# Scaling turned features in place of weights, with the projection in row-split runs and a new order of the prologue

## The chip, the cores and the metric

The kernel runs on one core of a Trainium2 chip. The metric is the device time of one execution in microseconds (us). A run of the changed kernel always has runs of the kernel before beside it on the same chip. PE is the matrix engine, DVE the vector engine, ACT the scalar engine, POOL the general engine, and SP the engine that issues the transfers.

## The reference, cut to what matters

One transformer block with linear attention, S = 2048 tokens, D = 576, 32 heads of 18, hidden width 4608:

```python
mod = (silu(c) @ w_mod).reshape(1, 6, 1, -1)         # sa, ca, ga, sb, cb, gb
h = layernorm(x) * (1 + ca) + sa
q, k, v = h @ wqkv                                   # cut: the split into heads
phi(u) = [softmax(u @ w_phi), softmax(-u @ w_phi)]   # per head, 18 + 18 features
kv, z = sum_s phi(k) v, sum_s phi(k)
o = (phi(q) kv) / (phi(q) z + 1e-6)
x = x + ga * (o @ wo)
h = layernorm(x) * (1 + cb) + sb
x = x + gb * (relu(h @ w1) @ w2)
```

The layer norm's factor (1 + ca) can be put into the weights of K, Q and V, or into the features that they multiply. That choice is the heart of the change.

## The kernel before

The sixteen token tiles of 128 rows pass a *prologue* (modulation, K, V, kv, Q, attention of the first two tiles) and then eight *blocks* of two tiles, each with a first layer (L1, `w1`) and a second layer (L2, `w2`). The prologue is one hand-written order of small jobs, which gives every engine its queue:

```python
ORDER = """
Z11 sx sd rp sc FK ca Z2 fs0 fsr frr fra2 sh frd4 fra0 fra1 bn1 fs3 bn0 fs1 Z1 fra3 shc sa0 wsd2 KR:0 fsd4 fs2
...                                                                            # cut
"""
```

`Zn` is n filler matmuls on zeros; `sc` and `sh` are the modulation's scale and shift products; `FK` folds `w_phi` into K's weights; `fs`, `fsd`, `fr` copy the fold out, scaled or raw; `ws` scales V's weights. The modulation products have one-column matmuls, and `idle` puts a filler in front of every five:

```python
def mods(w, outs, width, bank, idle=None):
    o = PS[:, bank, :] if isinstance(bank, int) else bank[:, 0, :]
    for k, wm in enumerate(w):
        for ci in range(NC):
            if idle is not None:
                spin(1, idle)
            for ck in range(NC):
                pe.matmul(o[0:width, k * NC + ci:k * NC + ci + 1], lhsT=wm[0:R, ck, ci * width:(ci + 1) * width],
                          rhs=siluc[0:R, ck:ck + 1], start=(ck == 0), stop=(ck == NC - 1))
# ...
"sc": lambda: mods([wsc], None, R, 7, idle=6),
"sh": lambda: mods([wsh], None, R, 7, idle=6),
```

Inside the blocks, hooks put the next block's attention between the matmuls:

```python
def in_l1(g, u):
    if not more:
        return
    if (g, u) in ((0, -1), (0, 1)):            # finish a query tile, fetch a later one
        q = t0 + max(u, 0)
        q_fin(q)                               # POOL steps, then the query's turning transfer
        if q + NL < NT:
            q_in(q + NL)
    if (g, u) in ((1, 2), (2, 1)):             # attention, then its turning transfer
        ...
def in_l2(pos):
    if pos in (1, 4): ...                      # projection, ten matmuls; residual; statistics
    if pos in (2, 6): ...                      # second norm; h's turning transfer
    if pos == 12:
        hb = h2[:, (b + 1) % 2]
        for ci in range(NC):
            dve.tensor_scalar(out=hb[:, ci, :], in0=hb[:, ci, :], scalar1=mod2[:, 1, ci:ci + 1],
                              scalar2=mod2[:, 0, ci:ci + 1], op0=ALU.mult, op1=ALU.add)
```

The softmax here doesn't subtract the row's maximum and nothing guards it: scores larger than these inputs give would overflow.

## Time and profile before

| | before |
|---|---|
| median of 3 runs | 393.02 us (391.85 to 393.25) |
| span of the profiled run | 390.7 us |
| PE busy | 383.8 us, 98% |
| first layer of block 0 starts (chain of waits) | 93.68 us |
| a block, from first layer to first layer | 37.05 us, all seven alike |
| last block's start to the end | 37.67 us |

The span is thus three pieces: 93.68 + 7 x 37.05 + 37.67 = 390.7 us.

### The profile page before, as it was taken

To read this page: it belongs to the slowest core of one execution; us is meant where nothing else is said; L and a number is where in the kernel's file an instruction comes from. 1 tells how busy PE (TensorE), PEld (TensorE's weight loads), DVE (VectorE), ACT (ScalarE), POOL (GpSimd) and SP (SyncE) were. 2 spreads that over 40 slices of the span, in tenths; PEclk is the share of its full clock that TensorE was granted. 3 is DMA by queue.
4 is the path that set the end of the run, shared out by engine and by line. 5 is a ranking of instruction groups with operands and counts; after the bars stand their busy time and mean duration, and the time that the engine had idled before them with its cause. 6 is when DMAs were issued, how large, how long until landed. Compare 5 with 4: busy or idle time off the path is not lost.

```text
span 390.7 us, 8908 instructions
## 1 busy us (share of the span) xinstructions
PE 383.8 (98%) x3693; PEld 311.7 (80%) x3693; DVE 244.3 (63%) x452; ACT 157.9 (40%) x360; POOL 142.3 (36%) x199
## 2 busy tenths in 40 slices
PE   8999999999999999999999999999999999999995
PEld 4778888878887888788888878887888788878874
DVE  0889998854879746573755567458555664653221
ACT  1798779699531233124213510531143123312510
POOL 2155858741101510740164045306510641072045
PEclk9999999999999999999999999999999999999999
DMA  7999739795732151125313311450143124010001
GB/s 291 418 420 403 274 133 354 178 306 161 189 65 35 47 121 20 35 61 109 35 27 83 80 35 32 107 65 19 47 93 35 24 69 51 18 34 33 3 0 32
DMA packets 49515, 44.36 MB, mean 114 GB/s; under 512 B 39361, under 2 KB 42050, under 8 KB 48706
## 3 DMA queue, kind: packets, MB, share of 16 engines
q1 hardware_dynamic: 49186, 43.59, 39.6%
q8 instruction: 29, 0.48, 0.5%
q10 hardware_dynamic: 288, 0.19, 0.2%
q14 instruction: 12, 0.10, 0.1%
HBM read 27.97 MB, written 6.49 MB: 88 GB/s over the span
## 4 chain that ended last, share of the span: by engine, by line
PE 86%; POOL 6%; ACT 2%; DVE 2%; DMA 2%; issue 1%; SPq 0%; POOLq 0%; DVEq 0%; ACTq 0%
PE PS L683 33%; PE PS L742 29%; PE PS L274 9%; PE PS L410 5%; PE PS L690 5%; POOL wo_sb L637 2%; PE PS L235 2%; PE PS L391 1%; ACT RT L279 1%; POOL RH L754 1%; DMA gatd<-gt 1%; PE PS L324 1%; POOL RT L291 1%; DMA ga_row<-gatd 1%; DVE st L240 1%
## 5 line engine op out<-in xcount | busy, mean ns | idle before, releaser
L683 PE MATMUL PS<-h,R 128*128 128x256 bf16 x1152 | 133.5, 273 | 0.0
L683 PEld LDWEIGHTS <-R 128*128 128x128 bf16 x1152 | 109.8, 98 | 17.5 <-issue 5.1
L742 PEld LDWEIGHTS <-RH 128*128 128x128 f16 x864 | 84.5, 98 | 21.8
L728 POOL TENSOR_TENSOR yt<-yt,gb_row 128x288 f32<-128x288 f32 x23 | 16.8, 731 | 167.0 <-DVE yt L727 167.0
L742 PE MATMUL PS<-R,RH 128*128 128x288 bf16 (+1 forms) x576 | 75.6, 286 | 0.0
L697 ACT ACTIVATE RH<-PS 128x256 f16<-128x256 f32 x72 | 27.7, 384 | 114.0 <-PE PS L690 107.4
L699 DVE SCALAR_TENSOR_TENSOR RH<-PS,RH 128x256 f16<-128x256 f32 x72 | 30.1, 419 | 68.2 <-ACT RH L697 68.2
L279 ACT ACTIVATE RT<-PS,rs 128x576 bf16<-128x576 f32 x64 | 43.0, 750 | 7.5 <-PE PS L274 7.1
L698 ACT ACTIVATE RH<-PS 128x512 f16<-128x512 f32 x72 | 42.9, 595 | 7.8 <-PE PS L683 6.5
L746 ACT ACTIVATE RS<-PS 128x288 f32<-128x288 f32 x24 | 9.9, 411 | 75.9 <-PE PS L742 75.9
L742 PE MATMUL PS<-RT,RH 128*128 128x288 f16 x288 | 37.9, 286 | 0.0
L274 PE MATMUL PS<-RH,R 116*128 116x288 bf16 x240 | 31.8, 286 | 0.5 <-ACT RH L631 0.5
L754 POOL TENSOR_TENSOR RH<-RH,RT 128x2304 f16<-128x2304 f16 x7 | 31.8, 4548 | 0.0
L274 PE MATMUL PS<-RH,RT 116*128 116x288 bf16 x240 | 31.7, 286 | 0.0
L274 PEld LDWEIGHTS <-R 116*128 116x128 bf16 x240 | 22.9, 98 | 6.4 <-issue 0.7
L274 PEld LDWEIGHTS <-RT 116*128 116x128 bf16 x240 | 22.7, 98 | 5.5
L420 DVE TENSOR_SCALAR xn<-x_sb,mv,rs 128x576 bf16<-128x576 bf16 (+1 forms) x28 | 22.4, 842 | 7.3 <-ACT rs L415 7.3
L729 POOL TENSOR_TENSOR x_sb<-yt,x_sb 128x288 bf16<-128x288 f32 x31 | 22.8, 737 | 5.9 <-DVE yt L725 4.1
L240 DVE BATCH_NORM_STATS2 st<-x_sb 128x6 f32<-128x288 bf16 x60 | 24.2, 445 | 0.5
L410 PE MATMUL PS<-wo_sb,oT 128*128 128x288 bf16 x160 | 22.6, 286 | 0.2 <-POOL wo_sb L637 0.2
L284 DVE TENSOR_REDUCE Rk<-RT 128x64 f32<-128x1152 bf16 x16 | 21.2, 1332 | 1.4 <-ACT RT L279 1.4
L284 DVE TENSOR_REDUCE Rq<-RT 128x64 f32<-128x1152 bf16 x16 | 21.5, 1342 | 0.0
(115 smaller groups left out, 414.2 us busy)
## 6 DMA issues: line engine op xcount, KB each, us to landing
R<-in_w1a_dram SPq DMA_DIRECT2D x4, 1152.0 KB
eqd<-RT SPq DMA_DIRECT2D x14, 288.0 KB, 5.8
RT<-eqd SPq DMA_DIRECT2D x14, 288.0 KB, 2.7
R<-in_w2a_dram SPq DMA_DIRECT2D x3, 864.0 KB, 10.4
R<-in_w2b_dram SPq DMA_DIRECT2D x2, 1296.0 KB, 10.9
out_dram<-x_sb SPq DMA_DIRECT2D x15, 144.0 KB, 3.3
RT<-in_xT_dram SPq DMA_DIRECT2D x2, 640.0 KB
x_sb<-in_xk_dram SPq DMA_DIRECT2D x3, 288.0 KB
```

The lines of the kernel that those rows point to most:

```text
L240: dve.bn_stats(out=s[:, hf, :], in_=x_sb[:, t, hf * HD:(hf + 1) * HD])
L274: pe.matmul(pr[:, k, 0:HD], lhsT=xt(t, ck), rhs=w[0:R, ck, k * HD:(k + 1) * HD], start=(ck == 0), stop=(ck == NC - 1))
L279: act.activation(out=E.rearrange("p (b h s e) -> p b h s e", b=2, s=2, e=DH)[:, :, :, s, :], in_=pr[:, :, 0:HD].rearrange("p b (h e) -> p ...
L284: dve.tensor_reduce(out=Rr, in_=E.rearrange("p (c e) -> p c e", e=DH), axis=AXX, op=ALU.add)
L410: pe.matmul(pr[:, k, 0:HD], lhsT=oT[:, t % 2, ci, :], rhs=wo_sb[:, ci, k * HD:(k + 1) * HD], start=(ci == 0 and not add_x), stop=(ci == NC ...
L683: pe.matmul(PS[:, 2 * u + hf, n * 256:n * 256 + 256], lhsT=w1a[:, ci, jj * P:(jj + 1) * P], rhs=hb[:, ci, :], start=(n == 0 and ci == 0), ...
L697: act.activation(out=A11[:, j, :], in_=lo[:, :, 0, :], func=ACT.Relu)
L698: act.activation(out=A2[:, j, :, :], in_=PS[:, 2 * u + 1, :].rearrange("p (n s f) -> p n s f", n=2, s=2), func=ACT.Relu)
L699: dve.scalar_tensor_tensor(out=U3[:, j, :], in0=lo[:, :, 1, :], scalar=0.0, in1=A11[:, j, :], op0=ALU.max, op1=ALU.subtract)
L729: pool.tensor_tensor(out=x_sb[:, t, c], in0=y, in1=x_sb[:, t, c], op=ALU.add)
L742: pe.matmul(PS[:, bank, 0:HD], lhsT=am[:, j, :], rhs=bm[:, j, :], start=first and j == 0, stop=(j % 9 == 8), skip_group_check=True)
L754: pool.tensor_tensor(out=A12, in0=A12, in1=U2, op=ALU.subtract)
```

## The change

The intent: fewer small operations ahead of K (features are scaled in place of weights), ten projections in each of which two of ten matmuls are replaced by a pair of half-height ones that run at the same time, no identity matmuls for the residual, a last epilogue in two halves, and a new order throughout. The diff, cut to its core:

```diff
 ORDER = """
-Z11 sx sd rp sc FK ca Z2 fs0 fsr frr fra2 sh frd4 fra0 fra1 bn1 fs3 bn0 fs1 Z1 fra3 shc sa0 wsd2 KR:0 fsd4 fs2
+Z11 sx sd rp sc bn1 Z2 ca bn0 FK sa0 sp0 fra0 frd4 sh fra3 frr fra1 xd0 T0:2 fra2 Z2 bn3 Tc0 Ka0:0 shc bn2
 ... (all lines of the order are new)
-    def mods(w, outs, width, bank, idle=None):
+    def mods(w, width, bank):
             for ci in range(NC):
-                if idle is not None:
-                    spin(1, idle)
 ...
+    def x_scale(t, eng):                        # the turned features of two tiles, times 1 + ca
 ...
+            if (g, u) in ((0, 0), (0, 2)):      # in_l1, blocks 2 to 6
+                attend(t0 + u // 2)
+            if g and u == "rest":
+                wo_rest(t0 + g - 1, pair(3))    # the pair of 64-row matmuls, in an existing row-split run
+            if g and u == 0:
+                wo_full(t, pair(3))             # eight full matmuls
+                add_res(t, pair(3))
 ...
+                if b and (g, u) == (1, 0):      # in_l1, block 1
+                    q_next(t0 + 2)
 ...
+            if b > 1 and pos in (4, 9) or b == 1 and pos == 9:   # in_l2
+                q_next(t0 + 2 + pos // 9)
 ...
+        if b + 1 == NB:                         # last epilogue: in halves
+            dve.tensor_tensor(out=yl[:, H4:HD], in0=PS[:, Z, H4:HD], in1=SS[:, 1, H4:HD], op=ALU.add)
+            dve.tensor_copy(out=yl[:, 0:H4], in_=SS[:, 1, 0:H4])
+            pool.tensor_tensor(out=yl, in0=yl, in1=gb_row[:, HD:D], op=ALU.mult)
+            pool.tensor_tensor(out=yl, in0=yl, in1=x_sb[:, t, HD:D], op=ALU.add)
+            dve.tensor_tensor(out=yt[:, 0, c], in0=PS[:, bank, c], in1=gb_row[:, g], op=ALU.mult)
+            dve.tensor_tensor(out=x_sb[:, t, g], in0=yt[:, 0, c], in1=yl[:, c], op=ALU.add)
```

The fillers inside the two modulation products are gone, and the preparation of later query tiles (`q_next`) has moved from the start of L1 into L2 in blocks 2 to 6, while block 1 has two such steps more than before.

## The prediction

> **What bounds the kernel now.** I read first the page's busy table and its slices, for the engine that is never idle; then the windows by stage, for whether that holds in every stage; then the chain that ended last, for what one unit of work costs on that engine; last the timeline of the first 15 us and of the last 5 us, where the slices show holes.
>
> From the page (busy us, share, instructions; then tenths in 40 slices):
>
> ```profile
> span 390.7 us, 8908 instructions
> ...
> PE 383.8 (98%) x3693; PEld 311.7 (80%) x3693; DVE 244.3 (63%) x452; ACT 157.9 (40%) x360; POOL 142.3 (36%) x199
> ...
> PE   8999999999999999999999999999999999999995
> ```
>
> Only the first and last slices have PE below nine tenths. The windows by stage (PE, PEld, DVE, ACT, POOL busy, clock, DMA share, GB/s) agree:
>
> ```profile
> 14.10:30.00 15.90, 15.09 (x178) 12.42 (x179) 14.59 (x28) 13.83 (x36) 7.56 (x21) 1.00 1.02 421
> 30.00:58.00 28.00, 28.00 (x342) 22.83 (x341) 26.88 (x50) 21.54 (x58) 17.63 (x45) 1.00 0.68 264
> ...
> 76.00:93.50 17.50, 17.31 (x167) 14.02 (x165) 11.17 (x23) 16.54 (x31) 6.58 (x5) 1.00 0.76 248
> 93.50:387.00 293.50, 293.29 (x2730) 240.26 (x2727) 171.25 (x320) 86.90 (x201) 94.33 (x91) 1.00 0.27 56
> ```
>
> From 93.5 to 387 us, three quarters of the span, PE lacks 0.2 us and the clock is full: there only PE work that is removed can pay. Before that DVE (26.88 of 28.00) and ACT (16.54 of 17.50) run close behind it.
>
> Busy PE is no proof of a tight stream, so I checked rates in the chain of waits (start, length, what, count):
>
> ```profile
> 167.78 3.06 PE PS L683 x28
> 170.84 0.76 PE PS L690 x12
> ...
> 188.05 1.23 PE PS L410 x10
> 189.28 3.31 PE PS L742 x27
> ```
>
> A 256-column matmul takes 3.06/28 = 0.109 us, a 288-column one 3.31/27 = 0.123 us. The row-split run (L690, twelve matmuls on 64 rows, so six pairs) takes 0.76 = 6 x 0.109 + 0.10 us. One block, 130.73 to 167.78, is 37.05 us; its items add up to that.
>
> The opening has the holes. PE and DVE timeline:
>
> ```profile
> 13.04 0.38 PE L235 MATMUL PS<-zero 128*128 128x512 bf16 x1
> 14.16 1.40 PE L268 MATMUL PS<-R,RS 116*100 116x288 bf16 x10 [0.75 <-DVE RS L614]
> ...
> 13.89 0.13 DVE L614 CAST RS<-PS 116x5 bf16<-116x5 f32 x1
> ```
>
> The first useful dense matmuls (K's bias rows) start at 14.16, behind a DVE queue that was full from 10.5 us: two evictions of the fold's rest (L618, L620), one raw fold (L453), then two layer-norm statistics.
>
> **What the Trainium skill says.** "TensorE: Matmul & The Clock Gate", section Back-to-back issue gap, gives N/2.4 + 2.5 ns for a warm isolated stream: 109.2 ns at N = 256, 122.5 at 288. The trace agrees (109, 123). The same section says that 128-column matmuls with their weight loads sustain only about 81 ns; the trace differs: the 25 fold matmuls of 126 columns take 1.46 us, 58 ns each, so I use the trace. "TensorEngine Tiling (Array Packing)", section Key Properties, says a change of tiling mode drains the engine, while tiles of one mode run in parallel; the 0.10 us excess above is that, and it says why the new projection remainder is put inside an existing row-split run. "VectorE: DVE Perf Modes", section The perf-mode tier table, puts a bf16 scalar multiply from SBUF at 4x and any PSUM source at most at 2x: here the 116x576 SBUF scale (L519) ran three in 0.93 us, the 116x504 PSUM scale (L444) took 0.73 us. That favours scaling features in SBUF.
>
> **The change, part by part.** (1) Scaling the turned features in place of the weights. Removed: of K's fold the scaled copies (four ACT at 0.65-0.68, one DVE at 0.73, one DVE remainder at 0.53), five V scalings on DVE (0.3 to 0.37 each), five scaled Q copies on ACT (0.73 each). Added for eight pairs of tiles: two on DVE (5 x about 0.2-0.35, between a 116x576 scale and L820's 1.78/5 for 256 columns: 1 to 1.8 us a pair), three on ACT (5 x about 0.4 = 2 us, from L697's 0.384 for 256 columns) and three on POOL (1280 elements; L291's 576 take 1.17 us and L754's 2304 take 4.5, so 2.5 us). In total ACT is about even (-6.3 + 6), DVE loses about 3 us and gains 2 to 3.6, and POOL, with room, gains 7.5. PE does no less. What counts is the start. My walk in queue order: the modulation weights land at 6.1 as before; the early token tile lands 0.7 us behind (288 KB at 410 GB/s), so statistics run on a DVE that today has only three tiny operations before 9.07; the 25 scale matmuls without idle fillers end near 7.9 in place of 8.9. The fold's weights land 0.7 us later than they did, near 8.6, so the fold stays at about 8.9 to 10.4. ACT then copies four fold chunks in 2.3 us, to about 12.7; K's first four chunks run to 13.2-13.8; the bias rows start near 13.7 (before 14.16). The half-row evictions let tile 1's exponentials start near 17.2, where the first started at 18.44. Then ACT and DVE feed PE: by my walk PE is about 0.6 us ahead at 27 us. I take 0.6 us from here.
>
> (2) The end of the prologue. Four identity matmuls with the residual go: 4 x 0.123 = 0.49 us of PE. Two ACT copies back to SBUF (0.65 each) go, in a stage where ACT is at 16.54 of 17.50; DVE gets two adds at 0.75 with room. The gate row is sent earlier, so the wait of the first projection for POOL's weights (0.35 us from 82.28 to 82.63) should go. Against that stand three filler matmuls after K's start (3 x 0.22), which I expect inside waits. Sum of PE work from 14.16 to 93.52: 77.2 us counted (480 projections x 0.1225 = 58.8, the rest kv, folds, rows, turns), elapsed 79.4; so 2.2 us of stalls are all that better order can win there. I take 0.6 + 0.49 + 0.35 = 1.4 us together.
>
> (3) Projection in row-split runs, for tiles 6 to 15: ten matmuls of 0.123 become eight, plus one parallel pair of 0.123 without a new mode change. Saved: 0.123 x 10 = 1.23 us, all on the path. For blocks 2 to 6 the attention and projection move from the second layer into the first. Room: attention's output is ready about 5.7 us into the block, its turning DMA takes 2.6, so it lands near 8.5; the first use is at 10.5. The bank pair is read out by DVE about 1.3 us before the second layer writes it. No stall expected, and none removed, since there is none.
>
> (4) The tail. From the timeline:
>
> ```profile
> 384.42 2.37 PE L742 MATMUL PS<-R,RH 128*128 128x288 bf16 x18
> ...
> 386.89 0.46 DVE L777 TENSOR_TENSOR yt<-PS,gb_row 128x288 f32<-128x288 f32 x1 [1.75 <-PE PS L742]
> 387.49 0.46 DVE L778 TENSOR_TENSOR x_sb<-yt 128x288 bf16<-128x288 f32 x1
> ```
>
> The last 18 matmuls become 36 of 144 columns (36 x 62.5 ns = 2.25 us, +0.05). The first half's DVE pair hides under the second half; what is left exposed is two operations on 144 columns at about 0.31 us (0.46 less 144/0.96 ns). 1.06 us becomes about 0.75. Net 0.3 us. The 2.7 us of the last store stay.
>
> Sum: 1.4 + 1.23 + 0.3 = 2.9 us; with a little for order effects that I did not count, 3.3. 393.0 - 3.3 = 389.7.
>
> **Rivals.** First, the front is bound by the loads: DMA share is 1.0 from 4 us on, and loading x earlier only pushes the fold's weights back. For it: the fold already starts as its weights come. Against: DVE, not DMA, ended the last wait (L614). Then the prologue gains only (2), some 0.8 us, and the time is about 390.6. Second, feature scaling becomes a new wait: DVE is 96% busy from 30 to 58, ACT gets three times 2 us in the same stretch, and a POOL scale of 2.5 us stands in front of the small POOL steps (L594, L598) on which V's eviction waits. PE would stall some 1 to 2 us: 391 to 392. Third, the tight end: the last turned tile now stands only one projection (1.23 us) before the first layer; its evictions need 1.0 us on DVE, and on ACT they queue behind a tile's exponentials (1.3 us). That costs up to 0.7 us once. Fourth, the projection waits for its turning DMA inside the first layer: at 1 us a tile over ten tiles that would be +10 us, the only road to slower; the 2 us of room speaks against it. Fifth, upward: the start comes a full 2 us earlier and all stalls go; then 3 + 2.2 + 0.49 + 1.23 + 0.3 = 7.2 us at the very most.
>
> **Range and chances.** Low end 387.4: the start 1.5 us better than my walk and most stalls gone. High end 391.5: rivals one to three in part. Faster by over 2% means under 385.2, a gain of 7.8, beyond the 7.2 that I can find: 0.04. Slower by over 2% needs the fourth rival: 0.02.
>
> **What would show it.** Right: the first-layer stage of block 0 starts near 92 us (93.5 before); blocks 2 to 6 last 36.8 us where they lasted 37.05; in those blocks the second and third row-split runs last about 0.88 us in place of 0.76; last PE to end shrinks by 0.3; PE still lacks under 0.5 us in the blocks. Wrong: idle PE ended by ACT or POOL on the feature tiles between 15 and 58 us (second rival), idle ahead of L690's successor ended by the turning DMA (fourth), or K's first matmul no earlier than before (first). A gain above 6 us would mean stalls that busy PE hides and that my count of 2.2 missed.

## More of the kernel before

In the timeline of PE before (start, length, engine, line, operation, count), the one-column products (L251) alternate with fillers (L235), and the dense fold (L438) follows:

```profile
7.74 0.38 PE L251 MATMUL PS<-siluc,R 116*116 116x1 bf16 x5
7.98 0.38 PE L235 MATMUL PS<-zero 128*128 128x512 bf16 x1
...
8.89 1.58 PE L438 MATMUL PS<-RS,R 126*116 126x126 bf16 x25
```

## The result

The changed kernel takes 398.75 us (median of 4 runs, 397.67 to 399.26), the kernel before in the same rounds 392.51 us. The ratio is 1.0155, with a 95% interval of 1.0123 to 1.0187. Ratios here are the mean time of one kernel's runs over that of the other's of the same rounds, so not quite the ratio of the medians. A gain of 3.3 us was predicted and a loss of 6.2 us came: within 2%, but 7 us above the range.

From the page after, the busy table and two rows of the slices (PE busy, and the clock that PE was granted, in tenths):

```profile
span 397.2 us, 8949 instructions
...
PE 386.0 (97%) x3700; PEld 312.9 (79%) x3701; DVE 237.1 (60%) x463; ACT 157.1 (40%) x376; POOL 146.5 (37%) x202
...
PE   7999999999999998999999999999999999999996
...
PEclk8599999999999999999999999999999999999999
```

PE is as busy as before. The row to look at is the last one: the second slice (9.9 to 19.9 us) has half the clock, where before has nines throughout. Put into the three pieces by the starts of the first layers in the chain of waits:

| piece | before | after | difference |
|---|---|---|---|
| to the first layer of block 0 | 93.68 | 96.34 | +2.66 |
| block 0 | 37.05 | 37.29 | +0.24 |
| blocks 1 to 6 | 222.30 | 225.88 | +3.58 |
| last block and end | 37.67 | 37.69 | +0.02 |
| span | 390.7 | 397.2 | +6.5 |

Of blocks 1 to 6, block 1 lost 1.40 us, block 2 lost 0.53 and the others 0.40 to 0.42 each.

**The opening.** PE's timeline after, which answers to the one of before:

```profile
5.98 1.49 PE L247 MATMUL PS<-siluc,R 116*116 116x1 bf16 x25 [0.69 <-DMA R<-in_wsc_dram]
...
8.54 2.80 PE L432 MATMUL PS<-RS,R 126*116 126x126 bf16 x25 [0.50 <-DMA R<-in_wkT_dram]
11.14 2.63 PE L247 MATMUL PS<-siluc,R 116*116 116x1 bf16 x25
```

The same 25 fold matmuls take 2.80 us in place of 1.58 in this view, and in the window 8 to 17 us the mean granted clock is 0.50 (before 1.00) at almost the same busy time of PE, 8.28 against 8.25 us of 9.00. A busy share does not show a slow clock.

**Blocks 2 to 6.** The chain of waits after, at the start of block 3 (start, length, what, count):

```profile
207.93 1.79 DVE h L857 x3
...
210.57 2.89 PE PS L671 x25
```

Three of the 28 first-layer matmuls have run; the other 25 wait for DVE, which scales the five parts of h. Before, the whole run starts unhindered. In the timeline after, and then in that of before:

```profile
205.64 1.17 POOL L287 TENSOR_TENSOR RT<-RT,ratq 128x576 bf16<-128x576 bf16 x1
...
207.93 2.85 DVE L857 TENSOR_SCALAR h<-h,mod 128x256 bf16<-128x256 bf16 x5
...
208.22 0.73 POOL L717 TENSOR_TENSOR yt<-yt,gb_row 128x288 f32<-128x288 f32 x1
...
209.03 1.41 POOL L718 TENSOR_TENSOR x_sb<-yt,x_sb 128x288 bf16<-128x288 f32 x2
...
209.49 0.67 PE L671 MATMUL PS<-h,R 128*128 128x256 bf16 x3
```

```profile
240.16 1.78 DVE L820 TENSOR_SCALAR h<-h,mod 128x256 bf16<-128x256 bf16 x5
...
240.32 0.77 POOL L729 TENSOR_TENSOR x_sb<-yt,x_sb 128x288 bf16<-128x288 f32 x1 [0.64 <-DVE yt L725]
...
241.72 3.22 PE L683 MATMUL PS<-h,R 128*128 128x256 bf16 x28
```

The five scalings took 2.85 us where they took 1.78, although nothing about them changed. What changed is POOL beside them: two query steps (L287), moved into L2, have pushed POOL's later work (L717, L718) under the scalings. The views of the two lines give the single scalings (min, median and max in ns), before and then after:

```profile
L820 DVE TENSOR_SCALAR h<-h,mod x5: 334/335/761, 240.2 to 241.6; 128x256 bf16<-128x256 bf16 x5
L857 DVE TENSOR_SCALAR h<-h,mod x5: 339/764/885, 207.9 to 210.4; 128x256 bf16<-128x256 bf16 x5
```

By itself a scaling takes about 0.34 us. Before, one POOL instruction (240.32) runs beside the five, and one scaling takes 0.76. After, three POOL instructions do, and three scalings take 0.76 to 0.89. Each of these long scalings ends 0.08 us after a POOL instruction ends. The same holds for all 137 scalings of over 0.6 us at the block ends of the 13 profiled runs that have them on DVE. So DVE stands until the POOL instruction is over, and even the old 1.78 us holds one such wait. This agrees with the Trainium skill, "SBUF — State Buffer", section "SBUF: two separate sides": DVE, when it uses both of its ports, and POOL lock one shared pair of ports for a whole instruction each, and the other blocks. The longest case is in both kernels: h's normalisation (128x576), 0.42 us by itself, takes 2.68 beside POOL's multiplication of 4.55 us (at 233.96 before, at 164.16 after); before, it cost PE nothing.

The new projection itself works as designed. Its waits aside, three undisturbed matmuls take 3 x 0.109 = 0.33 us from 209.49, so the other 25 could start at 209.82; they start 0.75 us later. Blocks 3 to 6 last 37.45 to 37.47 us: 0.75 lost and 0.34 gained on 37.05.

**Block 1.** SP's queue, from the timeline after (SP issues in the order written):

```profile
147.25 1.89 SPq L346 DMA_TRANSPOSE RE<-RT  x1
...
151.19 0.33 SPq L335 DMA_DIRECT2D RT<-eqd  x1
151.61 2.04 SPq L399 DMA_TRANSPOSE oT<-o_sb  x1
```

The attention output `o_sb` is complete at 147.41 us (DVE's last operation on it starts at 146.65 and lasts 0.76). Its turning could have been issued then; it was issued at 151.61, after a query's turning and a fetch into the same buffer that has to wait for that turning. PE pays at the projection:

```profile
155.12 1.40 PE L404 MATMUL PS<-wo_sb,oT 128*128 128x288 bf16 x10 [1.22 <-DMA oT<-o_sb]
```

The Trainium skill, "Perfetto Trace Analysis", section "DMA Instruction — HWDGE (DVE, Sync)", places the wait for semaphores in the issuing sequencer, which is free for the next instruction only after it has issued. The trace agrees: 4.2 us of delay for a transfer whose data was ready. The late projection has a sequel: h's own turning lands late for block 2, at 171.27 us in the chain of waits, and DVE starts to scale h only at 171.37, 0.55 us before the first layer's first matmul, where blocks 3 to 6 have 1.56. That goes with block 2's 0.53 us.

**The tail.** The timeline of DVE after, for the last epilogue in halves:

```profile
393.29 0.31 DVE L774 TENSOR_TENSOR yt<-PS,gb_row 128x144 f32<-128x144 f32 x1 [1.67 <-POOL x_sb L718]
...
394.20 0.31 DVE L775 TENSOR_TENSOR x_sb<-yt,RE 128x144 bf16<-128x144 f32 x1
```

The first half did not hide under the matmuls of the second: it writes the scratch `yt[:, 0]`, which POOL (L718) still reads, so all four operations stand at the end.

### The profile page after: what moved, and what is told of

It is laid out like the page before. It is cut to its first block, busy times and chain, and to the rows that moved or that the text cites. A ratio compares the mean times of both kernels' runs of the same rounds, so it can differ in the third digit from the quotient of the medians.

```text
span 397.2 us, 8949 instructions
## 1 busy us (share of the span) xinstructions
PE 386.0 (97%) x3700; PEld 312.9 (79%) x3701; DVE 237.1 (60%) x463; ACT 157.1 (40%) x376; POOL 146.5 (37%) x202
## 4 chain that ended last, share of the span: by engine, by line
PE 83%; POOL 4%; DVE 4%; DMA 4%; ACT 2%; issue 2%; SPq 0%; POOLq 0%; DVEq 0%
PE PS L671 32%; PE PS L731 24%; PE PS L270 12%; PE PS L678 5%; DVE h L857 3%; PE PS L804 3%; PE PS L404 2%; PE PS L387 2%; DMA R<-in_wkT_dram 2%; ACT RT L275 1%; POOL RH L743 1%; PE PS L320 1%; DMA h<-xn 1%; PE PS L247 1%; POOL RT L287 1%
## 5 line engine op out<-in xcount | busy, mean ns | idle before, releaser
L671 PEld LDWEIGHTS <-R 128*128 128x128 bf16 x1152 | 111.1, 98 | 19.0 <-issue 5.9
L731 PEld LDWEIGHTS <-RH 128*128 128x128 f16 x846 | 82.8, 98 | 20.8
L717 POOL TENSOR_TENSOR yt<-yt,gb_row 128x288 f32<-128x288 f32 x23 | 16.8, 729 | 187.4 <-DVE yt L716 187.4
L731 PE MATMUL PS<-R,RH 128*128 128x288 bf16 (+1 forms) x558 | 72.4, 286 | 0.0
L687 DVE SCALAR_TENSOR_TENSOR RH<-PS,RH 128x256 f16<-128x256 f32 x72 | 28.8, 413 | 62.8 <-ACT RH L685 62.8
L270 PE MATMUL PS<-RH,R 116*128 116x288 bf16 x240 | 33.8, 291 | 0.1
L716 DVE TENSOR_TENSOR yt<-PS,RS 128x288 f32<-128x288 f32 x23 | 10.4, 452 | 29.7 <-POOL RH L743 24.0
L238 DVE BATCH_NORM_STATS2 st<-x_sb 128x6 f32<-128x288 bf16 x64 | 25.9, 447 | 3.6 <-DMA x_sb<-in_xk_dram 3.1
L718 POOL TENSOR_TENSOR x_sb<-yt,x_sb 128x288 bf16<-128x288 f32 x31 | 22.4, 730 | 2.4 <-DVE yt L714 0.6
L678 PE MATMUL PS<-h,R 64*128 64x256 bf16 x288 | 19.9, 271 | 0.0
```

What stands on the lines that cost most here:

```text
L238: dve.bn_stats(out=s[:, hf, :], in_=x_sb[:, t, hf * HD:(hf + 1) * HD])
L270: pe.matmul(pr[:, k, 0:HD], lhsT=xt(t, ck), rhs=w[0:R, ck, k * HD:(k + 1) * HD], start=(ck == 0), stop=(ck == NC - 1))
L671: pe.matmul(PS[:, 2 * u + hf, n * 256:n * 256 + 256], lhsT=w1a[:, ci, jj * P:(jj + 1) * P], rhs=hb[:, ci, :], start=(n == 0 and ci == 0), ...
L678: pe.matmul(PS[:, 2 * u + hf, n * 256:n * 256 + 256], lhsT=w1b[b0:b0 + 64, j * P:(j + 1) * P], rhs=hb[b0:b0 + 64, 4, :], start=False, stop ...
L687: dve.scalar_tensor_tensor(out=U3[:, j, :], in0=lo[:, :, 1, :], scalar=0.0, in1=A11[:, j, :], op0=ALU.max, op1=ALU.subtract)
L718: pool.tensor_tensor(out=x_sb[:, t, c], in0=y, in1=x_sb[:, t, c], op=ALU.add)
```

## The experiments

Twelve kernels ran. All gave correct results. The theory had three parts: (A) without fillers the clock goes cold; (B) the moved query steps hold POOL, and through it DVE, in blocks 2 to 6, and SP's queue in block 1; (C) scratch in the tail. The rivals: the new order of the prologue is slow by itself; h comes too late by its transfer; the new projection costs more than it saves. "First layer" below is the start of block 0's first layer in the chain of waits.

| run | this | before beside it | ratio, 95% interval |
|---|---|---|---|
| e1 front only | 394.49 | 392.21 | 1.0048 (1.0015 to 1.0082) |
| e2 loop only | 394.91 | 392.21 | 1.0065 (1.0050 to 1.0080) |
| e3 fillers back | 394.77 | 392.21 | 1.0064 (1.0044 to 1.0084) |
| e4 query steps moved | 393.49 | 392.21 | 1.0036 (1.0015 to 1.0058) |
| e5 = e3 + e4 | 390.91 | 392.31 | 0.9962 (0.9950 to 0.9975) |
| e6 = e5 + tail | 390.77 | 392.31 | 0.9958 (0.9945 to 0.9972) |
| e7 h on ACT | 395.35 | 392.31 | 1.0077 (1.0034 to 1.0120) |
| e8 first filler set | 396.08 | 392.31 | 1.0095 (1.0081 to 1.0109) |
| e9 old front, mended loop | 390.60 | 392.17 | 0.9957 (0.9942 to 0.9973) |
| e10 weight scaling late | 391.48 | 392.17 | 0.9975 (0.9962 to 0.9988) |
| e11 and query step early | 391.59 | 392.43 | 0.9983 (0.9969 to 0.9997) |
| e12 before, no fillers | 394.20 | 392.17 | 1.0045 (1.0032 to 1.0058) |

### e1_front_only and e2_loop_only: which half loses

e1 is the changed prologue with the blocks and tail of before; e2 is the prologue of before with the changed blocks and tail.

```diff
 # e1: everything up to the first block from the changed kernel, the rest from the kernel before
 # e2: the other way round
```

> The changed prologue (feature scaling, loads, order) with the block loop and tail of before. Theory A (my reading of the two traces): the prologue of the change loses by itself, the first layer of block 0 starts near 96.3 us against 93.6, and the blocks stay at 37.05 us; total about 2.8 us over before, some 395.4. Rival B (all the loss sits in the loop, the late start is made good later by slack in the loop): within 0.5 us of before. My prediction on record would want 1.4 us under before.

> The prologue of before with the changed block loop and tail. Theory A: loop and tail lose by themselves, about 1.9 us in block 1, 0.4 us in each of blocks 2 to 5, gain 0.5 in the last moved block; total about 3.5 us over before, some 396.1, with DVE's feature scaling at the end of each block taking 2.85 us where it took 1.78. Rival B (loop loses only because of a PE clock or DMA state inherited from the prologue): within 0.5 us of before. My prediction on record would want 1.5 us under before.

Both halves lose by themselves. In e1 the first layer starts at 95.84 us, with a mean clock of 0.62 in 8 to 17 us, and its blocks are 37.05 us again. In e2 it starts at 92.97 us, and first to last block takes 261.65 us where before takes 7 x 37.05 = 259.35: +2.3 us in the trace. So there is no single cause. By the ratios the two halves make up 0.0113 of the 0.0155; e1's four runs spread over 3.3 us, which can cover the rest. The loss expected in block 1 of e2, 1.9 us, was 0.37 (1.40 after the change, 0.98 in e3), so it depends on the state in which the prologue leaves the queues.

### e3_fillers_back, e8_fill_first and e12_before_no_fillers: the clock

```diff
 # e3 (e8: the first of the two only, Z11 kept)
-    def mods(w, width, bank):
+    def mods(w, width, bank, idle=None):
             for ci in range(NC):
+                if idle is not None:
+                    spin(1, idle)
-        "sc": lambda: mods([wsc], R, 7),
-        "sh": lambda: mods([wsh], R, 7),
+        "sc": lambda: mods([wsc], R, 7, idle=6),
+        "sh": lambda: mods([wsh], R, 7, idle=6),
-Z11 sx sd rp sc bn1 ...
+Z12 sx sd rp sc bn1 ...
 # e12, on the kernel before
-        "sc": lambda: mods([wsc], None, R, 7, idle=6),
-        "sh": lambda: mods([wsh], None, R, 7, idle=6),
+        "sc": lambda: mods([wsc], None, R, 7),
+        "sh": lambda: mods([wsh], None, R, 7),
```

> The changed kernel with the idle fillers back inside the two modulation products and twelve fillers at the start. Theory A1: the cold clock of 8 to 17 us (0.50 in the trace) is what makes the prologue late: mean clock back to 0.999 and first layer of block 0 near 93.3 to 94, total about 396 to 396.5. Rival A2: the prologue is late because DVE and ACT feed it late and PE was only waiting while cold: clock 0.999, but first layer still at 95.5 or later, total about 398. One of the four timed runs of the changed kernel had clock 1.0 and was only 0.7 us faster than the others, which speaks for A2.

> The changed kernel with the five fillers back in the first modulation product only, eleven at the start. Theory A1a: it is the thin first product behind a gap of 0.7 us that lets the clock fall, so five fillers there suffice: no slice under 1.00 from 8 to 17 us, first layer of block 0 near 93. Rival A1b: the second product, as thin, or the wait for the fold's weights does it too: cold again from 11 us on or later, first layer at 94 to 96.

> Control: the kernel before, with nothing changed but the idle filler matmuls inside its two modulation products taken out. Theory (the fillers, not the order of work, hold the granted clock): the granted clock falls to about 0.5 to 0.8 of full in the stretch 8 to 17 us, the 25 fold matmuls take over 2 us in place of 1.46, and the first layer starts 1 to 3 us later than 93.68; median 393.5 to 395. Rival (the clock falls only with the new order, where K starts before its bias rows and the fold comes early): clock stays 1.0, time within 0.5 us of before.

With the fillers back (e3) the clock in 8 to 17 us is 1.00, the fold takes 1.60 us in PE's timeline, K starts at 12.83 us in place of 14.72, and the first layer starts at 92.86 us in place of 96.34. By the ratios, 1.0155 less 1.0064 of 392.5, the time falls by 3.6 us (2.3 to 2.8 were expected). With fillers in the first product alone (e8) the clock is 1.00 too and the ratio falls by 0.0060, or 2.4 us; e8 still stood 0.86 us at 61 us for another cause (below), which e3 did not. Its loop losses remain, as they should.

The control says the same from the other side. The order of before with its fillers taken out (e12) loses 0.45%, and its first layer starts at 94.98 us; its clock in 8 to 17 us is 0.69, and PE's timeline reads:

```profile
5.80 1.49 PE L251 MATMUL PS<-siluc,R 116*116 116x1 bf16 x25 [0.63 <-DMA R<-in_wsc_dram]
7.59 2.80 PE L438 MATMUL PS<-RS,R 126*116 126x126 bf16 x25 [0.30 <-DMA R<-in_wkT_dram]
```

The fold takes 2.80 us here as it did after the change. The rival that the new order is slow by itself falls: old order without fillers is cold, new order with fillers is warm. The Trainium skill, "TensorE: Matmul & The Clock Gate", section "What's actually happening", has PE at half clock unless it was active over a window of some 3.4 us, with a window that runs freely. A clock near half agrees: from the first start to the last, a fold matmul takes 106 ns on average after the change and in e12, and 58 before. So does the chance in it: in the five profiled runs without these fillers the clock in 8 to 17 us was 0.50 (after), 0.62 (e1), 0.69 (e12), 0.84 (e4) and 1.00 (e7, described below), and all but e12 share one prologue. All nine other profiled runs, with fillers in the first product at least, had 1.00. So without fillers the clock may fall, and with them it did not. Over all timed runs a kernel with fillers in the first product spread by 0.3 to 1.9 us, one without by 0.8 to 5.0 us.

That it is the clock that counts, and not the fillers as such, shows in the eight profiled runs with the changed prologue. From the start of the first layer in PE's timeline I subtract PE's wait near 61 us, which has another cause (e10 below). What is left is 95.5 us at a clock of 0.50 (after), 94.4 at 0.62 (e1), 92.9 at 0.84 (e4) and 92.7 at 1.00 (e7, without fillers), where the four with fillers have 92.7 to 92.9.

One thing stays open. The listed mean clock does not order the timed runs: e1 took 392.33 us at 0.998 and 395.66 at 0.999. Of the changed kernel's four runs one lists a mean clock of 1.000 and still took 398.38 us, and e7 ran from 392.78 to 397.79 us at listed clocks of 0.998 to 1.000. Either the listed clock misses a cold stretch, or something else varies too. One trace a kernel is kept; e7's is of a run of 394.32 us, and the slow ones have none.

### e4_q_moved and e7_h_on_act: the blocks

```diff
 # e4: query steps out of L2, and in block 1 behind the attention's turning
-                if b and (g, u) == (1, 0):
-                    q_next(t0 + 2)
+                if b and (g, u) in ((1, 2), (2, 2)):
+                    q_next(t0 + 1 + g)
+            if (g, u) == (1, 1):
+                q_next(t0 + 2)
             if (g, u) == (1, 2):
                 norm2(b, t0)
+                q_next(t0 + 3)
-            if b > 1 and pos in (4, 9) or b == 1 and pos == 9:
-                q_next(t0 + 2 + pos // 9)
 # e7: query steps left where the change has them, h scaled on ACT
-                    dve.tensor_scalar(out=hb[:, ci, :], in0=hb[:, ci, :], scalar1=mod2[:, 1, ci:ci + 1],
-                                      scalar2=mod2[:, 0, ci:ci + 1], op0=ALU.mult, op1=ALU.add)
+                    act.activation(out=hb[:, ci, :], in_=hb[:, ci, :], func=ACT.Identity, scale=mod2[:, 1, ci:ci + 1],
+                                   bias=mod2[:, 0, ci:ci + 1])
```

> The changed kernel with the query preparation taken out of the second layer (blocks 2 on) into the first layer, and in block 1 put behind the attention output's turning DMA. Theory C: POOL's query product beside DVE's scaling of h in the second layer holds DVE back (2.85 us in place of 1.78) and the DMA queue's in-order wait holds back the turning DMA in block 1; moved, blocks 2 to 6 last 36.8 us, block 1 37.05, and the total falls by 3.5 us, to about 395.2. Rival D: h is late because its own turning DMA lands late: the blocks stay at 37.4 us.

> The changed kernel with the five scalings of h at each block's end on ACT, the query preparation left where the change put it. Theory C1 (DVE's two-port mode is shut out while POOL works): on ACT the five take about 2.1 us whatever POOL does (0.42 each), h is ready near 0.65 + 2.1 us into the last product of 2.2 us, and the wait at each block's start falls from 0.75 to 0.3 us or less; blocks 3 to 6 last 36.8 to 37.1 us in place of 37.46. Rival D (h itself lands late, or POOL's own products are what L1 waits for): blocks stay at 37.4.

In e4 blocks 3 to 6 last 36.71 us, 0.34 under before, and the scalings of h are back to their old length, in the timeline of DVE:

```profile
203.75 1.78 DVE L858 TENSOR_SCALAR h<-h,mod 128x256 bf16<-128x256 bf16 x5
```

Block 1 lasts 37.23 us, and its attention output is no longer held at SP. By the ratios this is worth 1.0155 less 1.0036, 4.7 us (3.5 were expected), but a part of it may be the clock, which in this profiled run was 0.84. e5 against e3, both warm, gives a cleaner figure: 0.0102, or 4.0 us.

e7 separates B from its rival. POOL keeps its load and its place; only the engine that scales h is another. Its timeline has, for the same block:

```profile
202.70 2.56 ACT L857 ACTIVATE h<-h,mod 128x256 bf16<-128x256 bf16 x5
...
207.70 3.22 PE L671 MATMUL PS<-h,R 128*128 128x256 bf16 x28
```

h was there 5.0 us before the first layer's first matmul (202.70 against 207.70), so for these blocks the rival that its transfer is late falls. DVE begins 1.56 us ahead of the first layer, in the changed kernel (207.93 against 209.49) as before (240.16 against 241.72): what changed is how long it takes and not when it starts. Blocks 3 to 6 last 36.71 us here too. Block 1 keeps its wait, since the order at SP is unchanged. The time as a whole has little resolution, with a spread of 5 us; the blocks in the trace carry the verdict. That a scaling stands while a POOL instruction runs is shown by the single instructions above; that a pair of ports is what they share is the skill's explanation, which no run here tests.

### e5_fillers_q and e6_fillers_q_tail: together, and the tail

e5 is e3 and e4 in one. e6 adds:

```diff
-            dve.tensor_tensor(out=yt[:, 0, c], in0=PS[:, bank, c], in1=gb_row[:, g], op=ALU.mult)
-            dve.tensor_tensor(out=x_sb[:, t, g], in0=yt[:, 0, c], in1=yl[:, c], op=ALU.add)
+            dve.tensor_tensor(out=yt[:, 1, c], in0=PS[:, bank, c], in1=gb_row[:, g], op=ALU.mult)
+            dve.tensor_tensor(out=x_sb[:, t, g], in0=yt[:, 1, c], in1=yl[:, c], op=ALU.add)
```

> Fillers back and query preparation moved, tail as changed. If the losses found so far (cold clock 3.5 us in the fillers' trace, block stalls 4.7 us in the moved trace) are separate and add: first layer of block 0 near 92.9 us, blocks 2 to 6 at 36.7, total near 390.0 to 390.8, that is 1.5 to 2.2 under before. Rival: they share a cause and only one counts: about 393.

> As the one before, and the last epilogue writes its scratch to the other half of the scratch buffer. Theory E: in the change the first half's two DVE operations waited until POOL had read the scratch of the tile before (393.29 us, 1.1 us after their matmuls), so nothing of them was hidden; with the other half free they run under the second half's matmuls: from the last block's start to the end 37.35 us in place of 37.7, total 0.35 us under the kernel without this edit. Rival F: the store of the tile before it, which POOL releases late, ends last: no gain.

e5 stands 0.0193 of 392.5, 7.6 us, under the changed kernel. The two edits alone were worth 3.6 (e3) and 4.7 us (e4), together 8.3, so they add up within the intervals, which are near 1 us each. e5 is faster than before by 0.38%, e6 by 0.42%. The new scratch is worth 0.2 us in the trace (last block to end 37.53 us, where e5 has 37.73), 0.1 us in the medians, which lies inside the spread. In DVE's timeline of e6:

```profile
383.55 0.31 DVE L776 TENSOR_TENSOR yt<-PS,gb_row 128x144 f32<-128x144 f32 x1 [0.67 <-PE PS L774]
383.96 0.72 DVE L777 TENSOR_TENSOR x_sb<-yt,RE 128x144 bf16<-128x144 f32 x1
```

The wait for POOL is gone and PE ends it, as planned. The second operation, of two SBUF inputs, now lies beside POOL's last addition and takes 0.72 us in place of 0.31, but this costs nothing: the second half's first operation starts at 384.61 us, as its matmuls end (384.57). Half of the gain is missing at SP: the last store is issued at 385.45 us, 0.19 after its data is complete, behind another store (384.93, 0.42 us), where before it was issued 0.03 after.

### e9_old_front_q_tail: what is the changed prologue worth when warm?

The prologue of before (with its fillers), and the blocks and tail of e6.

```diff
 # e6 with everything ahead of the first block from the kernel before
```

> The kernel before's prologue with the changed loop, query preparation moved as in e4 and the last epilogue's scratch as in e6. It isolates parts (3) and (4) of the change, mended. Theory: first layer starts at 93.0 as in e2, blocks 2 to 6 at 36.71 (0.34 us under 37.05) and blocks 0 and 1 at about 37.2, so 5 x 0.34 + 0.14 (tail) = 1.8 us under the kernel before, some 390.5; then it equals e6 (390.77), which would say that the whole new prologue, when its clock is warm, is worth nothing. Rival: the prediction's own 1.4 us for the new prologue holds when it is warm, then this is 1 us or more slower than e6, about 391.8.

390.60 us, against 390.77 for e6; by their ratios 0.9957 and 0.9958. The whole changed prologue, once warm, is worth nothing that these runs can show; 1.4 us would be 0.0036, more than both intervals together leave room for. The rival that carried the prediction's 1.4 us falls. In the trace the blocks 3 to 6 are 36.71 us again; the first layer starts at 93.98 us in this profiled run, which with 391.27 us is one of the slower of six.

### e10_wo_late and e11_wo_late_qp_early: POOL at the end of the prologue

Six of the eight profiled runs with the changed prologue (after, e1, e4, e5, e7, e8) had a PE gap of 0.66 to 1.31 us at 61 to 64 us; e3 and e6 had none. In e5's timeline:

```profile
56.72 1.28 POOL L627 TENSOR_TENSOR wo_sb<-wo_sb,ga_row 128x576 bf16<-128x576 bf16 x1 [1.97 <-DMA ga_row<-gatd]
...
61.25 1.39 PE L272 MATMUL PS<-RH,RT 116*128 116x288 bf16 x10 [0.73 <-DVE RT L303]
```

POOL takes its work in order. It stood 1.97 us for the gate row's transfer, with steps behind it that V's eviction on DVE, and then PE, needed. e10 moves that weight scaling; e11 moves a query step too:

```diff
 # e10
-... K11:2 eK10 wo2 kv8 gbw ...
+... K11:2 eK10 kv8 gbw ...
-... Q3:1 wo4 sq2 kv15 eQ3 Q4:2 kz qp0 tp1 ...
+... Q3:1 wo4 wo2 sq2 kv15 eQ3 Q4:2 kz qp0 tp1 ...
 # e11, on e10
-... Q3:1 wo4 wo2 sq2 kv15 eQ3 Q4:2 kz qp0 tp1 ...
+... Q3:1 qp0 wo4 wo2 sq2 kv15 eQ3 Q4:2 kz tp1 ...
```

> e6 with one scaling of a projection weight by the gate row (the first, wo2) moved in POOL's queue from beside key tile 11 to beside query tile 3, after the gate row has long landed. Theory (POOL, which works in order, stood 1.2 to 2.0 us behind the gate row's DMA, and the V eviction behind it): no POOL wait for that DMA, no PE idle over 0.2 us between 55 and 70 us, first layer at 92.5 to 93.0; median 390.2 to 390.8, and less spread in the start of the first layer than between e5 (93.70) and e6 (93.01). Rival (the PE gaps of 0.7 to 1.3 us at 61 us come from DVE or ACT being late by themselves): the gap stays and the first layer starts at 93.5 or later. Risk: the weights' scaling now ends later and the first projection waits for it.

> e10 with one entry of the order moved: the first query tile's POOL step goes ahead of the two projection-weight scalings in POOL's queue. In e10 the gap at 61 us was gone (PE 18.00 of 18.00 in 58 to 76) but PE then stood 1.01 us at 80.8 for the turned query tile, whose POOL step came 2.5 us later, behind the two scalings. Theory (both gaps are POOL working strictly in order): neither gap is there, the first layer starts at 93.0 or earlier where e10 had 94.83 in the chain, and the median is 390.2 to 390.8, so at least 0.7 us under e10 and level with e6 and e9. Rival (the end of the prologue is bound by DVE or DMA, and POOL's order only shows where the wait falls): PE idles by 0.7 us or more somewhere else between 60 and 93 us and the median stays at 391.2 or above.

The gap at 61 us is gone in both (PE 18.00 of 18.00 us in the window 58 to 76). By itself that settles little, since e6, from which they start, had no gap in its trace either. The length of POOL's wait for the gate row settles it: in the six runs with a gap POOL waits 1.90 to 2.57 us, and in each of them PE's gap is POOL's wait less 1.24 to 1.26; in e3 and e6 POOL waits 0.82 and 1.23 us, and PE does not stand. Why the row lands later in some runs was not traced. Neither e10 nor e11 is faster than e6, and the gap only moved. PE's timelines of e10 and then of e11:

```profile
80.83 0.55 PE L389 MATMUL PS<-kvz,RE 128*128 128x76 bf16 x10 [1.01 <-DMA RE<-RT]
```

```profile
81.30 1.26 PE L406 MATMUL PS<-wo_sb,oT 128*128 128x288 bf16 x9 [1.36 <-POOL wo_sb L627]
```

In e10 the query tile's step queued behind two weight scalings and its turning came late; in e11 the scalings themselves came late. The hope for both (390.2 to 390.8) failed, and e11's rival was right: moving one step of POOL's queue moves where the wait falls. POOL holds 16.4 us of work in that window of 18, where before it holds 13.5. Less POOL work there, which might help, was not tried.

## Why the prediction was wrong

It said 389.7 us, and its range ended at 391.5. By its own steps:

- **(1) The start, "I take 0.6 us from here": this is the step that failed first.** It counted the missing fillers as time won ("end near 7.9 in place of 8.9") and assumed warm durations for what followed. The fillers were what kept the clock: e3, e8 and e12 show it. Cold, the start costs 2.7 us in the trace; the fillers are worth 3.6 us. The walk itself was good for a warm clock: in e3 K's bias rows start at 13.81 us (said 13.7), after the change at 16.64. Its costs of feature scaling were good: 0.28 us a step on DVE (said 0.2 to 0.35), 2.32 us a pair on POOL (said 2.5), 0.49 a step on ACT (said 0.4).
- **(2) The end of the prologue, 0.49 + 0.35.** Even warm, (1) and (2) together gave nothing measurable (e9 against e6) where 1.4 us were predicted. The 0.49 us of identity matmuls are gone, and so is the wait of the first projection for POOL's weights (0.35 from start to start before). But the gate row, sent earlier to remove that wait, became one itself: POOL stands for it, with the small steps behind it that V's eviction needs, and PE stands 0.66 us at 63.9 us. The second rival named the same small steps, but behind a feature scaling, for 1 to 2 us and between 15 and 58 us.
- **(3) The projection, 1.23 us.** The mechanism was right: two matmuls fewer, no new wait of its own. Each of blocks 2 to 6 gained 0.34 us once mended (37.05 to 36.71), so 1.7 us in all. Per tile, eight full matmuls take 0.99 us in place of 1.22 for ten, and the row-split run with the pair 0.88 (as predicted) in place of 0.76, so 0.11 us is gained where 0.12 was counted; twice that is 0.22, and the rest of the 0.34 was not traced. **The step that failed is "No stall expected".** It checked the rooms of the moved attention and projection, and not those of the query preparation that had to make way. That preparation landed on POOL beside DVE's scaling of h, 0.75 us a block, and at SP ahead of a transfer that was due. Put right, it is worth 4.0 us.
- **(4) The tail, 0.3 us.** It did not come (37.69 against 37.67), since "the first half's DVE pair hides under the second half" overlooked POOL's read of the scratch. With other scratch, 37.53: a gain of 0.14 us on before; the rest stands at SP, before the last store. The 0.31 us an operation was right.
- **Rivals.** The sign named for the first (loads), K no earlier than before, did show (14.72 us against 14.16), but from the cold clock: with fillers it is 12.83. The third (a tight end) came in part: block 0's first matmuls stand for ACT's evictions of h, so block 0 lasts 37.29 us in place of 37.05, and 37.58 in e4. The fourth, a projection that waits for its turning transfer, did occur, in block 1, where the projection had not moved: 1.22 us once and not in ten tiles. No rival named the clock, although the prediction itself noted "without idle fillers".

Mended, the change does what about half of the prediction said: e6 is 1.6 us under before (0.0042 of 392.3), of which the blocks account for 1.7. e5, e6 and e9 are level as the fastest of all these kernels.

## What to carry to other kernels

Before taking filler matmuls out, look at the granted clock in the stretch behind them, not at the busy share. When work moves, walk the queues of all engines at its new place for what now stands behind it, above all the in-order queues of POOL and SP, and check what DVE has to do while POOL is busy: a mean length can hide a wait that only the single instructions show. A gap that a reordering closes may open again elsewhere on the same engine, so judge by the time and not by the gap.

## What the Trainium skill lacked or had wrong

- "TensorE: Matmul & The Clock Gate" warns of idle gaps longer than its window of some 3.4 us. Here the longest gap in the opening, after PE's first matmul, was 0.69 us and PE was listed busy for 8.28 of 9.00 us, and still the clock was 0.50. That 25 one-column matmuls with such gaps about them, listed as busy, can lose the clock (four of five profiled runs), and that one 512-column filler for every five of them kept it (nine of nine), is not on the page; of short idles that lose the clock it has one other case, without their size.
- The same page's 81 ns for 128-column matmuls with their weight loads is too long for this case: 58 ns from start to start measured warm for 126 columns (106 cold).
- "SBUF — State Buffer" has the exclusive lock between DVE and POOL, but not that a blocked DVE instruction is listed as busy, nor a measured case of one: here it ends 0.08 us after POOL's (137 of 137), so a scaling of 128x256 took 0.76 us in place of 0.34 beside a POOL step of 0.7 us, and a normalisation of 128x576 took 2.68 in place of 0.42 beside one of 4.55 us.
- "Perfetto Trace Analysis" shows that the issuing sequencer waits, and not what follows for the transfers behind it: here 4.2 us for a transfer whose data was ready.
